# A filter block loaded and folded in two parts, nine small additions moved to GpSimd, eleven warm-up matmuls for fifteen, and a new order, in a gated long-convolution and token-mixing kernel

## The chip, the cores and the metric

One core of one Trainium2 chip runs the kernel. The metric is the device time of one execution in microseconds (us). The engines are TensorE (PE in the profile; its weight loads are listed apart as PEld), VectorE (DVE), ScalarE (ACT) and GpSimd (POOL). SyncE (SP) only issues DMAs here, and POOL issues a few of its own. All arrays are bfloat16; sums are made in float32.

## The reference, cut to what matters

S = 2048 positions, D = 640 channels, F = 1536 hidden units, a shift convolution of 4 taps.

```
x = A_q
g = sigmoid((x * gate_w).sum(-1))
# branch a: shift convolution, product, long causal convolution over S, product
k_shift = sum over t of k_pad[:, t:t+S, :] * shift_k[:, 3-t]
kv      = k_shift * v
y       = irfft(rfft(kv_pad) * rfft(ssm_k_pad)) + kv * ssm_D      # per channel, length 2S
a       = q * y
# branch b: layer norm over D, then an MLP over the positions
h = (x - mean) / sqrt(var + 1e-5)
u = gelu(einsum("bsd,sf->bdf", h, w1) + b1)
b = transpose(einsum("bdf,fs->bds", u, w2) + b2)
out = g * a + (1 - g) * b
```

## The kernel before, in words

**Long convolution.** The 2048 positions are cut into four blocks of n = 512, and so is the filter `ssm_k`. A block's transform is a product with cosine and sine tables on PE. The tables TFc, TFs, AFc and AFs are made in the kernel: GpSimd writes the rows of integers `frow` (iota), DVE multiplies them by a column and takes the result modulo the period (`idx`, L660, four operations for TFc/TFs and two for AFc/AFs), ACT takes sines. Two further small columns, `nyt`, come from DVE (L661).

For filter block i the steps are:

- `wnat_load` brings the block in, 128 channels x (5 columns of blocks x 512 values), 640 KB, into the buffer `wnat{i}`, which has 16 values more that a memset on POOL makes zero (they are read past the end by the reversed view).
- `w_turn(i)` folds it on DVE: `fw` is the block read forward and `bw` the block read backward; two wide operations (sum and difference, 128 x 1280 each) give the two parts e = 0 and e = 1 of `en`, and four operations of one value per row and block (`sam`) correct their first columns.
- For i = 0 and 1, PE turns `en` by products with the identity `idp`: four groups (e, k), each of five 128 x 128 products into one PSUM tile, which ACT or DVE copies to `eo` (`evict`, L1006 on DVE). For i = 0 the last group also adds `drow` (ssm_D). For i = 2 and 3 a DMA turns `en`.
- `w_freq(i)` multiplies `eo` by the tables (eight groups on PE), and ACT copies the results to `W{i}` (`Wo` for i = 1).

The product side is alike: `kv_block(i)` (shift convolution on PE with the small diagonal tables `dg`, evictions `ks`, a DMA that turns them to `kt`, products with v on DVE), `a_freq`, then `pair(j, m)` (products of A and W summed in Z, all DVE), `inverse(m)` (PE) and `epilogue(m)`.

**Token MLP.** The rows of x come in nine groups: tiles 0 and 1 alone, then pairs (2,3), (4,5), ... (14,15); a group is named by its first tile (ln0, ln1, ln2, ...). For each tile DVE takes the statistics of two halves (L919) and combines them (L921, buffer `mv`). For each group an addition of 1e-5 gives `vpe` (L923 through the helper at L660, DVE) and a power of -0.5 gives `rstd` (L924, POOL). Then DVE normalises (L661) or, for four of the tiles, ACT does, after a small DVE operation (`nmr`). `mlp1(s)` does two of the 12 tiles of F at a time (six sets), `mlp2(q)` two of the 16 tiles of S (eight sets, each with its own 768 KB block of w2, loaded through two buffers `w2_0` and `w2_1`).

**Ends.** The last scatter to the output (L728) takes tile 15, whose product (`mlp2(7)`, reversed weights `w2r1`) is made some groups before PE's end; the very last groups on PE are tile 14's, and DVE finishes that tile with two fused operations (L1327) from PSUM and two stores.

**Order.** Every operation is first recorded with a number in `_Plan`, and then issued in the hand-written list `ORDER` (L433 to L470). Each engine, SP's queue included, runs its own part of that list in the list's order; `_Tracker` puts in the semaphore waits for operands, and for buffers that are still in use. Each PE group takes one of four PSUM tiles (`pp0` to `pp3`) and holds it till its eviction. So what an engine waits for, it waits for in place: everything behind it in its own part of the list waits too. The numbers called cost and pr in the code (`cost=0.07`, `pr`) do not set the order here; the list does.

**Warm-up.** At the start PE multiplies a constant `wz` with itself, 15 matmuls of 128 x 512 (`NWARM`, L490 and L778), which nothing reads.

The part of the list that each engine sees at the start, by what it works on (wt1 = turning block 1, wf1 = its tables, and so on):

- PE: warm-up; the four turning groups of block 1; six table groups of block 1; the `drow` group of block 0; two more of block 1's; the other three of block 0; three shift convolution groups (cv0); block 0's table groups; then cv1 and the first set of the MLP.
- DVE: constants; four `idx`; statistics of ln1; an `idx` and two `nyt` and another `idx`; block 1's difference and sum; then statistics of ln14, ln12 and ln6 among block 1's corrections; block 0's folds as the 37th and 38th operation.
- POOL: three constants and `ncol_i` first, `frow` as the 9th and 10th operation.
- SP: x of ln1, block 1 of the filter (640 KB), `shd`, x of ln14, ln12 and ln6, `drow`, block 0 of the filter, x of ln8, and further x.

Of the kernel before, what the change touches and what calls it, by code (L numbers as in the profile page):

```python
# [8 lines left out]
BF16 = mybir.dt.bfloat16  # L9
# [3 lines left out]
ALU = mybir.AluOpType  # L13
# [409 lines left out]
def _checked(items, offs, base, top):  # L423
# [49 lines left out]
def _build(nc, A_q, A_k, A_v, A_shift_k, A_ssm_k, A_ssm_D, B_x, B_w1, B_b1, B_w2, B_b2, gate_w, out):  # L473
# [16 lines left out]
    NWARM = 15  # L490

    with ExitStack() as es:
# [14 lines left out]
        def buf(name, shape, dtype, t0, t1):  # L507
            spec.append((name, list(shape), dtype, t0, t1))
# [56 lines left out]
        for i in range(P):  # L565
            buf(f"wnat{i}", [128, DC * n + 16], BF16, (0, 0, 42, 52)[i], (26, 28, 52, 60)[i])
# [103 lines left out]
        def memset(ap, val, pr, eng="POOL"):  # L670
            return vop(eng, 0.03 + nel(ap) / 1200.0, lambda e: e.memset(ap, val), [], [ap], pr, kind="ms")  # L671
# [234 lines left out]
        for gi, (t0, cnt) in enumerate(groups):  # L906
# [16 lines left out]
            ts(b["vpe"][:, sl], b["mv"][:, sl, 1], 1e-5, None, ALU.add, None, pr, cost=0.07)  # L923
# [45 lines left out]
        def wnat_load(i, pr):  # L969
            dma(b[f"wnat{i}"][:, 0:DC * n].rearrange("p (c v) -> p c v", c=DC), dram(A_ssm_k, i * n, [[S, 128], [128 * S, DC], [1, n]]), f"wnat{i}", pr)  # L970

        brow = b["brow"]
# [35 lines left out]
        def w_turn(i):  # L1008
            plan.tag = f"wt{i}"
            wn = b[f"wnat{i}"]  # L1010
            en = b[f"en{1 if i == 1 else 0}"]
            eo = b[f"eo{i % 2}"]
            wnat_load(i, (-300.0, -280.0, -240.0, -180.0)[i])
            memset(wn[:, DC * n:DC * n + 16], 0.0, 0.3)

            def sam(v):
                return bass.AP(tensor=wn, offset=v, ap=[[DC * n + 16, 128], [n, DC], [1, 1]])

            fw = bass.AP(tensor=wn, offset=256, ap=[[DC * n + 16, 128], [-256, 2], [n, DC], [1, 128]])
            bw = bass.AP(tensor=wn, offset=256, ap=[[DC * n + 16, 128], [256, 2], [n, DC], [-1, 128]])  # L1020
            pr = 1.0 + 0.1 * i
            fo = i in FOLD
            tt(en[:, 0, :, :, :], fw, bw, ALU.add, pr)
            copy(en[:, 0, 0, :, 0:1], sam(256), pr, "DVE")
            tt(en[:, 1, :, :, :], fw, bw, ALU.subtract, pr)
            copy(en[:, 0 if fo else 1, 1, :, 0:1], sam(0), pr, "DVE")
            tt(en[:, 1 if fo else 0, 1, :, 0:1], sam(384), sam(128), ALU.add, pr)
            tt(en[:, 1, 0, :, 0:1], sam(384), sam(128), ALU.subtract, pr)
            if i in WDMA:
                dma(eo[:, :, :, :].rearrange("p e k (c d) -> p (e k c) d", c=DC),  # L1030
                    en[:, :, :, :, :].rearrange("p e k c u -> p (e k c u)"), f"wt{i % 2}", pr, turn=True)
            else:
                for e in range(2):
                    for k in range(2):
                        p_ = _PS()
                        xd = i == 0 and e == 1 and k == 1
                        mms = [(p_, c * 128, 128, en[:, e, k, c, :], ident, not xd or c in (0, 4), not xd) for c in range(DC)]
                        if xd:
                            mms += [(p_, c0, cn, ident[0:1, :], b["drow"][:, c0:c0 + cn], False, True)
                                    for c0, cn in ((0, 512), (512, 128))]  # L1040
                        pe([p_], mms, pr, cost=0.285 + (0.35 if xd else 0.0))
                        evict(WEV[i][2 * e + k], eo[:, e, k, :], p_)
# [395 lines left out]
```

## Time and profile before

| | |
|---|---|
| median of 3 runs | 190.6 us (190.5 to 192.65) |
| the profiled execution | 190.98 us |
| its span (first to last recorded instruction) | 189.2 us |
| PE busy | 178.8 us, 95% of the span, 1590 matmuls |
| DVE busy | 175.5 us, 93%, 246 instructions |
| ACT busy | 125.5 us, 66% |
| POOL busy | 35.2 us, 19% |
| DMA | 40.37 MB, mean 213 GB/s; HBM read 26.03 MB, written 7.54 MB |
| granted TensorE clock | 1.00 throughout |

How to read the profile's lines in the prediction: the rows of the stretches give for each stretch of the span its length, then for PE, PEld, DVE, ACT and POOL the busy time in it with the number of instructions in brackets, then the granted clock, the mean busy share of the DMA engines (a transfer counted where it ran can bring a stretch above 1), and GB/s. A row of the chain gives the time at which a step of the chain starts (us), how much of the chain it takes, the engine, what it writes and the line; "xN" are N instructions in a row. A row of the timeline gives start, busy time, engine, line, operation, out<-in, shapes, count, and in square brackets the idle time before it with what ended it. A row of the groups gives line, engine, operation, out<-in, shapes and count, then busy us and mean ns of one, then the idle time before them with what ended most of it.

### The profile page before, as it was taken

The page shows a single profiled execution, that of the slowest core. Times are in us where ns is not written, and L with a number is a line of the kernel's source. Part 1 is how long each engine was busy: PE and PEld are TensorE (multiplying, and loading weights), DVE is VectorE, ACT ScalarE, POOL GpSimd, SP SyncE. Part 2 cuts the span into 40 slices and gives each one's busy share as a digit, 9 for nine tenths or more (in the row PEclk, how much of TensorE's full clock was granted, in tenths as well). Part 3 has the DMA queues.
Part 4 walks back from the last instruction along what each step waited for, and adds up shares of the span by engine and source line. Part 5 has one row for each costly group of instructions (what it writes and reads, how often), then busy time and mean ns, then how long its engine had stood idle before and what let it go on. Part 6 is the DMA issues. An engine that isn't in the chain of part 4 may idle for free.

```text
span 189.2 us, 3940 instructions
## 1 busy us (share of the span) xinstructions
PE 178.8 (95%) x1590; PEld 123.0 (65%) x1590; DVE 175.5 (93%) x246; ACT 125.5 (66%) x202; POOL 35.2 (19%) x68
## 2 busy tenths in 40 slices
PE   7778899999999999999999999999999899999992
PEld 2345666566667757777767777777667577777771
DVE  7999999999999999999899999999999999997352
ACT  4978999787699489439823047706778482495930
POOL 8366076610000000101000000000005003110732
PEclk9999999999999999999999999999999999999999
DMA  5999999798996876787948998997988976979992
GB/s 155 315 325 272 130 152 282 221 222 190 236 326 129 196 202 181 151 248 164 232 67 221 231 243 197 219 242 205 309 280 224 225 226 221 232 215 240 175 166 69
DMA packets 81094, 40.37 MB, mean 213 GB/s; under 512 B 40051, under 2 KB 80884, under 8 KB 81076
## 3 DMA queue, kind: packets, MB, share of 16 engines
q1 hardware_dynamic: 78340, 37.18, 78.5%
q0 software_dynamic: 2736, 2.95, 9.3%
q8 instruction: 12, 0.20, 0.4%
q14 instruction: 6, 0.05, 0.1%
HBM read 26.03 MB, written 7.54 MB: 177 GB/s over the span
## 4 chain that ended last, share of the span: by engine, by line
PE 61%; DVE 22%; ACT 4%; issue 4%; DMA 4%; POOL 2%; POOLq 1%; DVEq 0%
PE pp L311 61%; DVE stats L919 6%; DMA w<-in_B_w_dram 4%; DVE v L653 3%; DVE en L653 3%; DVE es L653 2%; DVE idx L660 2%; DVE W L653 2%; ACT pq L691 1%; POOL rstd L924 1%; ACT xe L691 1%; DVE h L661 1%; DVE eo L1006 1%; DVE mv L921 1%; DVE A L653 1%
## 5 line engine op out<-in xcount | busy, mean ns | idle before, releaser
L311 PE MATMUL pp<-h,w 128*128 128x320 bf16 x384 | 57.1, 299 | 0.2
L311 PE MATMUL pp<-gT,w 128*128 128x320 bf16 x336 | 48.4, 299 | 0.9 <-DMA w<-in_B_w_dram 0.9
L311 PEld LDWEIGHTS pp<-h,w 128*128 128x128 bf16 x384 | 36.8, 98 | 15.9 <-issue 1.8
L311 PEld LDWEIGHTS pp<-gT,w 128*128 128x128 bf16 x336 | 32.6, 98 | 14.0 <-DMA w<-in_B_w_dram 1.4
L653 DVE TENSOR_TENSOR tt<-A,W 128x3840 bf16<-128x3840 bf16 (+2 forms) x16 | 27.8, 1738 | 0.3
L691 ACT ACTIVATE A<-pp 128x640 bf16<-128x640 f32 x32 | 21.3, 700 | 9.3 <-PE pp L311 9.3
L653 DVE TENSOR_TENSOR Z<-Z,tt 128x3840 bf16<-128x3840 bf16 (+1 forms) x14 | 26.2, 1868 | 0.2
L262 POOL DMA_DIRECT2D out_dram<-xe x3 | 3.8, 1252 | 73.0 <-DVE Z L653 68.4
L691 ACT ACTIVATE o<-pp,c,omg 128x640 bf16<-128x640 f32 x13 | 11.2, 881 | 6.8 <-PE pp L311 6.4
L691 ACT ACTIVATE ks<-pp 128x512 bf16<-128x512 f32 (+1 forms) x24 | 11.1, 518 | 6.1 <-PE pp L311 6.1
L691 ACT ACTIVATE gT<-pp,bf 128x640 bf16<-128x640 f32 x12 | 9.4, 792 | 8.2 <-PE pp L311 8.1
L691 ACT ACTIVATE xe<-xe,gg 128x640 bf16<-128x640 bf16 x16 | 12.7, 827 | 2.4 <-DMA xe<-rows_q 1.2
L919 DVE BATCH_NORM_STATS2 stats<-x 128x6 f32<-128x320 bf16 x32 | 13.7, 472 | 0.0
L653 DVE TENSOR_TENSOR Z<-A,W 128x3840 bf16<-128x3840 bf16 x6 | 12.8, 2154 | 0.9 <-PE pp L311 0.8
L691 ACT ACTIVATE pq<-pp 128x640 bf16<-128x640 f32 x16 | 10.3, 702 | 4.8 <-PE pp L311 4.8
L671 POOL MEMSET W<- 1x640 bf16 x4 | 2.7, 665 | 50.9 <-ACT nq L691 49.6
L691 ACT ACTIVATE W<-pp 128x640 bf16<-128x640 f32 x18 | 12.0, 722 | 0.1
L653 DVE TENSOR_TENSOR W<-W 128x2560 bf16<-128x2560 bf16 x8 | 11.9, 1486 | 0.0
L653 DVE TENSOR_TENSOR y<-pq 128x1280 bf16<-128x1280 bf16 (+1 forms) x10 | 6.6, 688 | 4.5 <-ACT pq L691 4.5
L311 PE MATMUL pp<-kT,dg 64*64 64x256 bf16 x320 | 10.5, 271 | 0.3 <-ACT Wo L691 0.3
L311 PE MATMUL pp<-eo,TFc 128*128 128x320 bf16 x48 | 8.9, 300 | 1.1 <-ACT TFc L691 1.1
L653 DVE TENSOR_TENSOR Z<-Z 128x1280 bf16<-128x1280 bf16 (+1 forms) x16 | 9.9, 653 | 0.1
(147 smaller groups left out, 303.6 us busy)
## 6 DMA issues: line engine op xcount, KB each, us to landing
w<-in_B_w_dram SPq DMA_DIRECT2D x24, 256.0 KB, 4.1
w<-in_B_w_dram SPq DMA_DIRECT2D x8, 768.0 KB, 5.1
wnat<-in_A_ssm_k_dram SPq DMA_DIRECT2D x4, 640.0 KB, 5.7
x<-in_A_q_dram SPq DMA_DIRECT2D x7, 320.0 KB, 6.3
out_dram<-o SPq DMA_DIRECT2D x6, 320.0 KB, 6.1
v<-in_A_v_dram SPq DMA_DIRECT2D x4, 320.0 KB, 4.5
rows_q<-in_A_q_dram SPq DMA_DIRECT2D x8, 160.0 KB, 3.2
xe<-in_A_q_dram SPq DMA_DIRECT2D x4, 320.0 KB, 5.8
```

What stands on the lines that cost most here:

```text
L262: ins = engobj.dma_start(out_ap, in_ap, accum_op=ALU.add)
L311: ins = self.nc.tensor.matmul(ps_ap, lhsT=lhsT, rhs=rhs, start=start, stop=stop)
L653: return vop(eng, c, lambda e: e.tensor_tensor(out_, in0, in1, op), [in0, in1], [out_], pr, kind="tt")
L660: return e.tensor_scalar(out_, in0, s1, None, op0=op0)
L661: return e.tensor_scalar(out_, in0, s1, s2, op0=op0, op1=op1)
L671: return vop(eng, 0.03 + nel(ap) / 1200.0, lambda e: e.memset(ap, val), [], [ap], pr, kind="ms")
L691: return e.activation(out_, src, func, **kw)
L919: vop("DVE", 0.393, (lambda o_, i_: lambda e: e.bn_stats(o_, i_))(o_, i_), [i_], [o_], pr, kind="bn")
L921: vop("DVE", 0.11, (lambda o_, i_: lambda e: e.bn_aggr(o_, i_))(o_, i_), [i_], [o_], pr, kind="ba")
L924: vop("POOL", 0.7, (lambda o_, i_, e_: lambda e: e.tensor_tensor(o_, i_, e_, ALU.pow))(b["rstd"][:, sl], b["vpe"][:, sl], bc(c_mh, [[8, 12 ...
L1006: vop("DVE", 0.74, lambda e: e.tensor_copy(dst, src()), [src], [dst], 0.3, ps=[p_], kind="ev")
```

## The change

- **Block 1 of the filter in two parts.** A new function `wnat_part` loads columns of blocks 0 to 2 (384 KB) and 3 to 4 (256 KB) with two DMAs. The buffer `wnat1` is 16 values longer: the second part begins 16 values later, and a second memset on POOL makes the gap zero. `w_turn(1)` does its six fold operations once for each part, twelve in all, on 3/5 and 2/5 of the values. The four turning groups on PE become eight (three products and two), two to one PSUM tile, which is copied out after the second. The memsets are recorded ahead of the loads.
- **vpe on POOL.** The nine additions of 1e-5 (L923) run on GpSimd, ahead of the powers that it runs already.
- **NWARM** is 11, not 15.
- **ORDER** is new from end to end: 865 operations, not 853. By engine, at the start:
  - PE: warm-up; the `drow` group of block 0 first, then its other three turning groups; then block 1's groups in halves (columns 0 to 2, then 3 to 4) mixed with table groups of both blocks and with cv0; cv1's first group stands right ahead of the MLP's first groups.
  - DVE: constants; four `idx`; two `nyt`; statistics of ln14 and ln0 among two `idx`; block 1's sum and difference of columns 0 to 2 as the 15th and 16th operation; block 0's folds as the 24th and 28th, with the corrections that its first PE group needs up to the 32nd; then block 1's columns 3 to 4 and the remaining corrections.
  - POOL: `frow`'s second half first, its first half fifth; the powers go in the order ln14, ln0, ln2, ln4, ln12, ln1, ln10, ln6, ln8 (before: ln1, ln14, ln2, ln10, ln12, ln0, ln4, ln6, ln8).
  - SP: x of ln14, `drow`, block 1 columns 0 to 2, x of ln0, block 0, `brow`, x of ln4, block 1 columns 3 to 4, `shd`, x of ln2, ln12, ln8, ln6, ln10, and x of ln1 after the first `kT`.
  - Later: on SP w2's block for q = 4 stands ahead of the two `rows_o0` stores (before: behind them), and w2's block for q = 2 stands, as before, right behind the turn of `kt1`, but ahead of that turn there is another of the three loads of v2 than before, and both wait for it. Behind tile 15's last PE group stand four PE groups of four weight tiles each (before: three).

The diff without the list:

```diff
-    NWARM = 15
+    NWARM = 11
...
-            buf(f"wnat{i}", [128, DC * n + 16], BF16, (0, 0, 42, 52)[i], (26, 28, 52, 60)[i])
+            buf(f"wnat{i}", [128, DC * n + (32 if i == 1 else 16)], BF16, (0, 0, 42, 52)[i], (26, 28, 52, 60)[i])
...
-            ts(b["vpe"][:, sl], b["mv"][:, sl, 1], 1e-5, None, ALU.add, None, pr, cost=0.07)
+            ts(b["vpe"][:, sl], b["mv"][:, sl, 1], 1e-5, None, ALU.add, None, pr, eng="POOL", cost=0.25)
...
+        def wnat_part(i, c0, c1, pr):
+            o0 = c0 * n + (16 if c0 else 0)
+            dma(b[f"wnat{i}"][:, o0:o0 + (c1 - c0) * n].rearrange("p (c v) -> p c v", c=c1 - c0),
+                dram(A_ssm_k, i * n + c0 * 128 * S, [[S, 128], [128 * S, c1 - c0], [1, n]]), f"wnat{i}_{c0}", pr)
...
-            wnat_load(i, (-300.0, -280.0, -240.0, -180.0)[i])
-            memset(wn[:, DC * n:DC * n + 16], 0.0, 0.3)
...
+            cuts = ((0, 3), (3, DC)) if i == 1 else ((0, DC),)
+            WR = DC * n + 16 * len(cuts)
+            if i == 1:
+                memset(wn[:, 3 * n:3 * n + 16], 0.0, 0.3)
+            memset(wn[:, WR - 16:WR], 0.0, 0.3)
+            for c0, c1 in cuts:
+                if i == 1:
+                    wnat_part(i, c0, c1, -290.0 + c0)
+                else:
+                    wnat_load(i, (-300.0, -280.0, -240.0, -180.0)[i])
+                cn = c1 - c0
+                o0 = c0 * n + (16 if c0 else 0)
...
+                fw = bass.AP(tensor=wn, offset=256 + o0, ap=[[WR, 128], [-256, 2], [n, cn], [1, 128]])
+                bw = bass.AP(tensor=wn, offset=256 + o0, ap=[[WR, 128], [256, 2], [n, cn], [-1, 128]])
+                tt(en[:, 0, :, c0:c1, :], fw, bw, ALU.add, pr)
...
+                tt(en[:, 1, :, c0:c1, :], fw, bw, ALU.subtract, pr)
...
+                ps = {}
+                for c0, c1 in cuts:
+                    for e in range(2):
+                        for k in range(2):
+                            if c0 == 0:
+                                ps[e, k] = _PS()
+                            p_ = ps[e, k]
...
+                            mms = [(p_, c * 128, 128, en[:, e, k, c, :], ident, not xd or c in (0, 4), not xd) for c in range(c0, c1)]
...
+                            pe([p_], mms, pr, cost=0.057 * (c1 - c0) + (0.35 if xd else 0.0))
+                            if c1 == DC:
+                                evict(WEV[i][2 * e + k], eo[:, e, k, :], p_)
```

More of the change, by code (lines that the diff above doesn't have):

```diff
@@ L970, in wnat_load @@
             dma(b[f"wnat{i}"][:, 0:DC * n].rearrange("p (c v) -> p c v", c=DC), dram(A_ssm_k, i * n, [[S, 128], [128 * S, DC], [1, n]]), f"wnat{i}", pr)
+        def wnat_part(i, c0, c1, pr):
+            o0 = c0 * n + (16 if c0 else 0)
+            dma(b[f"wnat{i}"][:, o0:o0 + (c1 - c0) * n].rearrange("p (c v) -> p c v", c=c1 - c0),
+                dram(A_ssm_k, i * n + c0 * 128 * S, [[S, 128], [128 * S, c1 - c0], [1, n]]), f"wnat{i}_{c0}", pr)
+        def wnat_load(i, pr):
+            dma(b[f"wnat{i}"][:, 0:DC * n].rearrange("p (c v) -> p c v", c=DC), dram(A_ssm_k, i * n, [[S, 128], [128 * S, DC], [1, n]]), f"wnat{i}", pr)
         brow = b["brow"]
@@ L1012, in w_turn, with sam @@
             eo = b[f"eo{i % 2}"]
-            wnat_load(i, (-300.0, -280.0, -240.0, -180.0)[i])
-            memset(wn[:, DC * n:DC * n + 16], 0.0, 0.3)
[L1016 to L1020, printed above, removed]
             pr = 1.0 + 0.1 * i
             fo = i in FOLD
[L1023 to L1028, printed above, removed]
+            cuts = ((0, 3), (3, DC)) if i == 1 else ((0, DC),)
[10 more added lines that the diff above has]
+                o0 = c0 * n + (16 if c0 else 0)
+                def sam(v):
+                    return bass.AP(tensor=wn, offset=v + o0, ap=[[WR, 128], [n, cn], [1, 1]])
+                fw = bass.AP(tensor=wn, offset=256 + o0, ap=[[WR, 128], [-256, 2], [n, cn], [1, 128]])
+                bw = bass.AP(tensor=wn, offset=256 + o0, ap=[[WR, 128], [256, 2], [n, cn], [-1, 128]])
+                tt(en[:, 0, :, c0:c1, :], fw, bw, ALU.add, pr)
+                copy(en[:, 0, 0, c0:c1, 0:1], sam(256), pr, "DVE")
+                tt(en[:, 1, :, c0:c1, :], fw, bw, ALU.subtract, pr)
+                copy(en[:, 0 if fo else 1, 1, c0:c1, 0:1], sam(0), pr, "DVE")
+                tt(en[:, 1 if fo else 0, 1, c0:c1, 0:1], sam(384), sam(128), ALU.add, pr)
+                tt(en[:, 1, 0, c0:c1, 0:1], sam(384), sam(128), ALU.subtract, pr)
             if i in WDMA:
@@ L1032, in w_turn @@
             else:
[L1033 to L1042, printed above, removed]
+                ps = {}
[5 more added lines that the diff above has]
+                            p_ = ps[e, k]
+                            xd = i == 0 and e == 1 and k == 1
+                            mms = [(p_, c * 128, 128, en[:, e, k, c, :], ident, not xd or c in (0, 4), not xd) for c in range(c0, c1)]
+                            if xd:
+                                mms += [(p_, d0, dn, ident[0:1, :], b["drow"][:, d0:d0 + dn], False, True)
+                                        for d0, dn in ((0, 512), (512, 128))]
+                            pe([p_], mms, pr, cost=0.057 * (c1 - c0) + (0.35 if xd else 0.0))
+                            if c1 == DC:
+                                evict(WEV[i][2 * e + k], eo[:, e, k, :], p_)
         ORD = (0, 1, 2, 3)
```

73 rows, old and new, of the table ORDER are left out of this document.

## The prediction

> **What bounds the kernel now.** I read the busy time by stretch first, then the chain of work that ended last in order of time, then the timeline of the first 36 us. The stretches (columns: length, then busy us and instructions of PE, weight loads, DVE, ACT, POOL; granted clock; DMA share; GB/s):
>
> ```profile
> 0.00:8.22 8.22, 5.84 (x15) 1.95 (x15) 6.50 (x20) 5.34 (x8) 5.63 (x34) 1.00 0.70 215
> 8.22:25.00 16.78, 13.95 (x179) 9.74 (x180) 16.78 (x55) 14.85 (x27) 6.74 (x9) 1.00 1.14 254
> 25.00:50.00 25.00, 24.32 (x231) 15.58 (x229) 24.86 (x53) 21.23 (x36) 10.09 (x13) 1.00 0.92 213
> 50.00:141.00 91.00, 91.00 (x852) 64.82 (x850) 89.61 (x72) 55.45 (x95) 1.24 (x2) 1.00 0.88 215
> 141.00:150.00 9.00, 8.11 (x61) 5.65 (x59) 9.00 (x8) 7.00 (x12) 2.38 (x2) 1.00 0.89 222
> 150.00:185.54 35.54, 35.54 (x262) 25.30 (x260) 27.97 (x42) 21.59 (x28) 8.12 (x8) 1.00 0.85 200
> 185.54:189.20 3.66, 0.00 (x1) 0.00 (x0) 0.74 (x2) 0.00 (x0) 1.01 (x1) 1.00 0.27 90
> ```
>
> PE's useful work starts at 8.22 and ends at 185.54. In those 177.32 us it idles 2.83 + 0.68 + 0.89 = 4.4 us, so its work is 172.9 us. The 5.84 us before are warm-up matmuls on a constant. DVE is full as well until about 170. The chain says the same by place:
>
> ```profile
> 6.48 1.69 DVE en L653 x3
> ...
> 49.74 92.22 PE pp L311 x858
> 141.96 6.96 DMA w<-in_B_w_dram
> 148.92 0.05 issue
> 148.96 23.55 PE pp L311 x172
> ```
>
> DVE sets the pace of the front (filter folds, layer norm statistics), PE that of everything from 49.7 on, with one DMA wait (the 0.89). The change removes no PE work but warm-up. So I do the sum on PE: when its useful work starts, how long it idles, at which rate it runs, and what follows its end.
>
> **Term 1: PE's first useful group.** Before, it transposes block 1 as soon as that is folded (8.22). In the new order PE begins with block 0's group (second part, second half, with drow), which needs block 0's two folds and two corrections, and DVE has more ahead of those. Path shares of such instructions, from the chain:
>
> ```profile
> 1.87 2.21 DVE idx L660 x4
> ...
> 5.54 0.49 DVE idx L660
> 6.02 0.07 DVE nyt L661
> 6.09 0.40 DVE idx L660
> ...
> 9.09 0.08 DVE en L653
> ...
> 9.22 1.19 DVE stats L919 x3
> 10.41 0.24 DVE mv L921 x2
> ...
> 12.65 1.48 DVE en L653 x2
> ...
> 17.66 0.72 DVE eo L1006
> ```
>
> The four index operations ended at 4.08; the two frow iotas now stand first and fifth on POOL instead of ninth and tenth, so I take 3.9. Then, on DVE: 2 nyt (0.14), 7 statistics at 0.40 (2.8), 2 index operations (0.89), the two folds of block 1's first three columns of blocks (0.74 each for five; 3/5 with the fixed part kept, 0.47: 0.94), 3 aggregates (0.36), block 0's two folds (1.48), four small ones (id2, the AFs column, two corrections at 0.08: 0.3). Together 6.9, so 10.8 against 8.22: **+2.6 us**. Do the loads carry it?
>
> ```profile
> 0.00:5.00 5.00, 3.93 (x10) 1.42 (x11) 3.60 (x11) 2.19 (x3) 3.98 (x26) 1.00 0.53 156
> 5.00:10.00 5.00, 3.55 (x27) 1.65 (x25) 4.68 (x18) 4.93 (x8) 1.66 (x8) 1.00 1.00 326
> ```
>
> Up to block 0's last byte SP now issues x 320, part one 384, x 160, block 0 640 KB: 1.5 MB. At these rates 0.78 MB are there by 5 us, the rest 2.3 us later, at 7.3; DVE asks for block 0 at 8.6. Part one (0.7 MB) is there by 4.7, asked for at 5.8. I cost the loads at nothing; the cover is about one us each.
>
> **Term 2: the idle after that.** Before, 2.83 us between 8.22 and 25, because block 1's groups run dry. Now both blocks' groups are mixed from the start. After the first four groups (1.9 us, to 12.7) PE needs block 1's last-corrected half: 5 small operations, two folds of the two remaining columns (0.35 each), one eviction (0.72), two more corrections, 2.05 us of DVE after 10.8, so 12.85: a gap of 0.2. From there DVE is ahead of PE for every group that I followed. The evictions on ACT remain a limit with four PSUM buffers; for those I leave 0.5, a choice. 2.83 becomes 0.7: **-2.1**.
>
> **Term 3: the rate.** The weight loads show when each warm-up matmul starts:
>
> ```profile
> 1.07 5.84 PE L311 MATMUL pp<-wz 128*128 128x512 bf16 x15 [1.07 <-DVE wz L671]
> ...
> 5.32 0.15 PEld L311 LDWEIGHTS pp<-wz 128*128 128x128 bf16 x1 [0.28 <-issue]
> ...
> 5.74 0.15 PEld L311 LDWEIGHTS pp<-wz 128*128 128x128 bf16 x1 [0.28 <-issue]
> ...
> 6.10 0.32 PEld L311 LDWEIGHTS pp<-wz 128*128 128x128 bf16 x2 [0.21 <-issue]
> ...
> 8.22 0.28 PEld L311 LDWEIGHTS pp<-idp,en 128*128 128x128 bf16 x5 [1.81 <-DVE en L653]
> ```
>
> One matmul in 0.42 us until about 6.0, then one in 0.2, though the clock column says 1.00 throughout: PE runs its first 4.9 us at half rate. Then comes a pause of 1.3 us, and the transposes after it run at full rate (five loads in 0.28). Eleven warm-ups end at 5.74, before the doubling, and then PE pauses for 5.1 us until 10.8. The trace has no such pause. Bounds: nothing lost (as after the pause of 1.3), or another 4.9 us at half rate, 2.45 us of work. The new state (never at full rate, pause four times as long) is nearer the start than the short pause, so I take the half rate. PE is busy 83% there (13.95 of 16.78), so 2.0, less the 0.7 of idle that a slower PE fills: **+1.3**.
>
> The Trainium skill (TensorE: Matmul & The Clock Gate, Part 1: The HAM clock gate) says that about 3.4 us of sustained activity open the full clock and an idle window of about 3.4 us closes it. The two spacings and the 1.3 us pause agree with it; a pause over 3.4 is not in this trace. By that rule the start at 10.8 is cold for 3.4 to 6.8 us, an estimated loss of 1.7 to 3.4 us before slack, and the sum would be about half a us higher.
>
> **Term 4: GpSimd's additions.** Nine additions leave DVE (0.03 to 0.13 us of path each, about 0.7) and the split adds six DVE instructions (four at 0.08, two fixed parts at 0.07, 0.46). DVE nets -0.3, which moves only PE idle that I have counted. On POOL the trace has no such addition; its neighbours:
>
> ```profile
> L924 POOL TENSOR_TENSOR rstd<-vpe,cst 128x2 f32<-128x2 f32 x7 | 5.3, 809 | 7.0 <-DVE vpe L660 6.9
> L924 POOL TENSOR_TENSOR rstd<-vpe,cst 128x1 f32<-128x1 f32 x2 | 1.1, 568 | 0.1
> L668 POOL CAST gwc<-bf 128x5 bf16<-128x5 f32 x1 | 2.4, 2395 | 0.0
> ...
> L668 POOL CAST hcol<-hcol_i 128x2 f32<-128x2 int32 x1 | 0.4, 357 | 0.0
> ```
>
> Between ln4's last aggregate and ln8's first normalisation DVE has 8 statistics, 6 aggregates, 9 normalisations and 2 nmr, 7.2 us; POOL has five powers at 0.81, one at 0.57 and six additions in it, 4.6 + 6v. It is late when v is over 0.43. Bounds of v: 0.1 (a memset's duration, a gain of nothing) and 2.4 (the 128x5 cast, 12 us late). The nearest in shape and type is the 128x2 cast, 0.36: 6.8 of 7.2, **0**. The extra memset of the gap waits for nothing on POOL.
>
> The Trainium skill (GPSIMD Engine Reference, 1. Specifications) says GpSimd shares SBUF interfaces with VectorE. The powers at 0.57 and 0.81 may show that; the sum stays as it is.
>
> **Term 5: the middle.** 0.68 + 0.89. The 0.89 was w2's block for q = 4, queued on SP behind two rows_o0 stores that waited for DVE; now it stands ahead of them, and the wait goes. Late next is the block for q = 2: it stands behind the kt transpose, which now stands behind a v load that waits for a later group of PE; about 0.7. I take 1.57 to 1.4: **-0.2**.
>
> **Term 6: the end.**
>
> ```profile
> 183.75 1.79 PE L311 MATMUL pp<-gT,w 128*128 128x320 bf16 x12
> 183.95 0.88 ACT L691 ACTIVATE o<-pp,c2x,omx 128x640 bf16<-128x640 f32 x1 [2.92 <-PE pp L311]
> ...
> 185.27 1.01 DVE L1327 SCALAR_TENSOR_TENSOR xe<-pp,omg,xe 128x320 bf16<-128x320 f32 x2
> 185.64 1.01 POOL L728 DMA_INDIRECT out_dram<-xe,rev  x1 [3.53 <-DVE xe L653]
> ```
>
> The last scatter hangs on PE's group that ends three groups of four before PE's end; in the new order four groups stand behind it, 0.54 us more. The other end (last fused operation, store) follows PE's end and limits the gain: **-0.5**.
>
> **Sum.** +2.6 - 2.1 + 1.3 + 0 - 0.2 - 0.5 = +1.1 us. It is made against the profiled execution (span 189.2, 190.98 us with what lies around it, 0.4 above the median of 190.6). On the median: **191.7 us**.
>
> **Rivals.** (B) The rate is full from 10.8 on: term 3 is 0, 190.4 us. For it: a shorter pause did no harm. Against: the doubling is not reached by 5.74. (C) The order leaves PE no idle time and the rate is full: 10.8 + 172.9 + 0.2, then 3.1, is 187.0 of span, -2.2: 188.4. Against: the old order, made in the same way, left 4.4. (D) GpSimd becomes the bound of the layer norm: an addition takes about 1.2 us beside DVE's two-input work, POOL is 4.6 us late with rstd, of which 1.5 hide behind PE's own lag: 194.8. It decides from v = 1.1 on. For it: the 2.4 us cast; against: every other small POOL row. (E) The change does not do what it says: the split gives no earlier fold that PE uses, since PE starts with block 0. That is in my sum already; if the fold of part one also waited for its load, PE would start another 1 us later: 192.7.
>
> **Chances.** Forecast 0.45, B 0.22, C 0.10, D 0.10, E 0.08; 0.05 for a wait that I have not seen. The measurement of this kernel can tell about 2% from no change, 3.8 us: faster means below 186.8, slower above 194.4. B, C, E and the forecast lie within; D and half of the unseen lie above. Faster 0.04, within 0.82, slower 0.14. The range goes from near C (188.4) to the line at 194.4, short of D: 188.6 to 194.4; the forecast's own is 190.4 to 193.
>
> **What would show it.** PE's first matmul on en at about 10.8 (term 1 wrong if at 8). The starts of its matmuls over 320 columns just after: 0.27 us apart is the half rate, 0.135 the full. Idle PE between 11 and 25 under 1 us (term 2). On POOL, additions near 0.36 and no DVE wait for rstd (term 4). PE waits for w2 at q = 2, not q = 4 (term 5). PE's end to the span's end 3.1 (term 6). Wrong altogether if PE idles several us after 50, where I followed only the main producers.

## The result and the profile after

The changed kernel takes 191.78 us (median of 22 runs, 190.83 to 193.43), the kernel before 190.41 us (22 runs). The ratio is 1.0062 with a 95% interval of 1.0044 to 1.0081: slower by 0.6%, some 1.2 us. The profiled execution of the changed kernel took 191.72 us with a span of 189.9 us, against 190.98 and 189.2. The two profiled executions thus lie 0.7 us apart, the medians 1.4: the account from the profile below covers the 0.7.

The stretches of the changed kernel, cut at PE's first and last useful group as in the prediction (columns as there):

```profile
0.00:12.07 12.07, 4.71 (x11) 1.49 (x12) 9.64 (x33) 9.03 (x13) 9.68 (x41) 0.87 0.82 249
12.07:25.00 12.93, 11.96 (x150) 9.15 (x154) 11.80 (x41) 10.53 (x18) 3.31 (x8) 0.86 1.07 242
25.00:50.00 25.00, 24.76 (x255) 16.72 (x248) 24.66 (x51) 20.99 (x37) 10.88 (x18) 1.00 0.81 189
50.00:141.00 91.00, 90.97 (x850) 64.67 (x848) 89.43 (x72) 55.47 (x95) 1.24 (x2) 1.00 0.92 215
141.00:150.00 9.00, 8.60 (x64) 5.99 (x63) 8.97 (x10) 4.74 (x7) 2.36 (x2) 1.00 0.94 226
150.00:186.62 36.62, 36.62 (x270) 26.11 (x268) 31.02 (x43) 25.71 (x35) 8.60 (x9) 1.00 0.91 207
186.62:189.90 3.28, 0.00 (x1) 0.00 (x0) 0.69 (x2) 0.00 (x0) 0.57 (x1) 0.98 0.32 108
```

PE's useful work starts at 12.07 instead of 8.22 and ends at 186.62 instead of 185.54. Between them PE idles 0.97 + 0.24 + 0.03 + 0.40 = 1.64 us (before 4.4), and is busy 172.9 us, as before. But the clock column is no longer 1.00. Cut at the places where it changes:

```profile
5.48:8.90 3.42, 0.30 (x2) 0.00 (x0) 3.42 (x11) 3.28 (x6) 2.74 (x8) 1.00 1.00 327
8.90:12.07 3.17, 0.00 (x0) 0.01 (x1) 2.65 (x12) 2.78 (x5) 3.08 (x10) 0.50 1.10 328
12.07:15.72 3.65, 3.65 (x28) 2.83 (x29) 2.55 (x11) 2.22 (x3) 1.84 (x4) 0.50 1.27 288
```

The warm-up opens the full clock at 5.48 and ends at 5.78; after 3.4 us with 0.30 us of work in them the grant falls to 0.50 at 8.90, and PE does its first 3.65 us of useful work at half rate.

Busy time alone doesn't tell where the time went, because at half rate PE is busy as well. So I compare when each kernel starts its n-th useful matmul; both have 1575. From the traces' starts, us:

| kernel | 1st | 101st | 401st | last | span |
|---|---|---|---|---|---|
| before | 8.23 | 20.94 | 48.61 | 185.24 | 189.2 |
| changed | 12.07 | 23.58 | 50.43 | 186.32 | 189.9 |
| changed, 36 warm-up matmuls (e1) | 11.68 | 21.94 | 48.42 | 184.14 | 187.7 |
| the same again (e10) | 11.94 | 22.17 | 49.23 | 185.37 | 188.9 |
| new front, old rest (e3) | 11.52 | 23.22 | 51.17 | 188.34 | 192.3 |
| old front, new rest (e4) | 8.23 | 20.93 | 48.60 | 184.55 | 188.1 |
| e1 without the split (e6) | 12.32 | 23.07 | 49.96 | 185.51 | 189.0 |
| before, 11 warm-up matmuls (e7) | 8.23 | 20.94 | 48.61 | 184.44 | 188.4 |

The changed kernel is 3.84 us late at its first matmul, 1.8 at the 401st and 1.1 at the last; 0.4 more comes back in the tail. Each row is one execution. Two executions of one kernel (e1 and e10) differ by 0.8 us at the 401st and by 1.2 at the last, so a difference of that size between two rows needs the runs beside it.

### The profile page after: what moved, and what is told of

Same layout as the page of the kernel before. It is cut to its first block, busy times and chain, and to the rows that moved or that the text cites. A ratio compares the mean times of both kernels' runs of the same rounds, so it can differ in the third digit from the quotient of the medians.

```text
span 189.9 us, 3933 instructions
## 1 busy us (share of the span) xinstructions
PE 177.6 (94%) x1586; PEld 124.1 (65%) x1586; DVE 176.2 (93%) x243; ACT 126.5 (67%) x202; POOL 36.6 (19%) x78
## 4 chain that ended last, share of the span: by engine, by line
PE 82%; DVE 6%; DMA 4%; POOL 3%; ACT 2%; issue 1%; DVEq 0%; POOLq 0%
PE pp L311 82%; DMA w<-in_B_w_dram 4%; DVE stats L920 3%; DVE idx L661 1%; POOL v L723 1%; DVE dg L1004 1%; POOL rstd L925 1%; ACT TFs L692 1%; ACT ks L692 1%; ACT o L692 0%; DVE eo L1015 0%; ACT adx L692 0%; DVE xe L1351 0%; POOL vpe L661 0%; POOL flp L661 0%
## 5 line engine op out<-in xcount | busy, mean ns | idle before, releaser
L311 PE MATMUL pp<-h,w 128*128 128x320 bf16 x384 | 57.8, 299 | 0.0
L311 PE MATMUL pp<-idp,en 128*128 128x128 bf16 x40 | 4.3, 277 | 6.3 <-DVE en L654 6.3
L311 PEld LDWEIGHTS pp<-kT,dg 64*64 64x64 bf16 x320 | 8.2, 105 | 3.0 <-issue 1.6
```

The costliest lines, as they stand in the source:

```text
L311: ins = self.nc.tensor.matmul(ps_ap, lhsT=lhsT, rhs=rhs, start=start, stop=stop)
```

## The experiments

The experiments ran on two chips. The kernel before took 191.13 us on the first (e1 to e4), 190.54 on the second (e5 to e8) and 190.53 there again (e9 to e11). The ratios are to the kernel before on the same chip; I hold these against each other, not the microseconds.

**e1: warm-up up to the first group.**

```diff
-    NWARM = 11
+    NWARM = 36
```

> The changed kernel with 36 warm-up matmuls instead of 11, so that PE is busy until about its first useful group at 12.07 us; nothing else differs. Theory A (the clock falls back in the pause, and PE's work behind it is paid for at half rate): the granted clock is 1.00 from about 6 us on, the transposes' matmuls start 0.053 us apart instead of 0.107, and the 1.8 us that the half rate cost (3.65 us of it, half lost) come back: 190.0 us against 191.8 for the changed kernel. Rival B (VectorE sets the pace of the front, so a faster PE only waits longer): the clock is full as well, but PE then waits for the fold dg, which ends at 23.07 whatever PE does; only the 1.1 us come back that VectorE waited for PE's groups: 190.7 to 191.8 us.

Measured: 189.7 us, 0.9947 of the kernel before (0.9914 to 0.9979). A second measurement beside another experiment (e10) follows below. Its stretches, then a row of its weight loads, then the same row of the changed kernel:

```profile
0.00:11.68 11.68, 9.95 (x36) 3.96 (x37) 9.64 (x33) 8.72 (x12) 9.29 (x37) 1.00 0.81 242
11.68:25.00 13.32, 12.26 (x171) 9.08 (x172) 13.29 (x47) 12.37 (x24) 5.61 (x14) 1.00 1.06 255
...
sum 187.70, PE 181.38 PEld 125.55 DVE 175.86 ACT 126.08 POOL 36.85; mean PE 25.91 PEld 17.94 DVE 25.12 ACT 18.01 POOL 5.26
```

```profile
11.68 0.28 PEld L311 LDWEIGHTS pp<-idp,en 128*128 128x128 bf16 x5 [1.15 <-DVE en L669]
```

```profile
12.06 0.45 PEld L311 LDWEIGHTS pp<-idp,en 128*128 128x128 bf16 x5 [7.03 <-DVE en L669]
```

Five loads take 0.28 us in e1 and 0.45 in the changed kernel, full and half rate. In e1 PE is busy 181.38 - 9.95 = 171.4 us behind its first group, 1.5 less than the 172.9 of the changed kernel (171.4 to 171.6 in all five executions of the new order at full clock: e1, e5, e6, e10, e11): that is the half rate. Theory A is shown. Rival B falls: at the 401st matmul e1 is 2.0 us ahead of the changed kernel, 0.4 of it from an earlier first group, and PE's wait for dg did not grow (0.8 us for 1.0). In e10's execution the lead is 1.2 us, which alone would not exclude rival B; but by the ratios its range is 1.0005 to 1.0062, and both measurements lie below it. VectorE did not hold PE back by as much as that, since it evicts two of block 0's groups itself and had waited for them; that wait (1.1 us in the changed kernel's list of waits) is gone in e1's.

**e2: fifteen warm-up matmuls, as before.**

```diff
-    NWARM = 11
+    NWARM = 15
```

> The changed kernel with 15 warm-up matmuls, as many as before; nothing else differs. Theory A (it is the pause before the first useful group that costs the clock, not the number of warm-up matmuls): the warm-up ends near 7 us, 5 us of pause are left, the granted clock still falls to 0.5 and lasts into 15 us: 191.4 to 191.8 us, no different from the changed kernel. Rival C (eleven warm-up matmuls are too few to open the clock, fifteen keep it open): the clock stays at 1.0 as in the kernel before, and the time is 190.0 to 190.7 us.

Measured: 191.54 us, 1.0024 (1.0001 to 1.0046), on the same chip as e1. Its clock falls in the same way:

```profile
5.00:10.00 5.00, 1.37 (x7) 0.40 (x5) 3.94 (x11) 3.81 (x7) 3.29 (x12) 1.00 1.01 319
10.00:15.00 5.00, 2.50 (x19) 1.80 (x20) 4.50 (x19) 4.11 (x7) 4.25 (x10) 0.68 1.32 332
15.00:20.00 5.00, 5.00 (x34) 3.50 (x32) 4.39 (x15) 3.09 (x6) 0.00 (x0) 0.64 0.95 235
```

So the four warm-up matmuls that the change took away are not what costs; the pause behind them is. Theory A holds and rival C falls: e2 is 0.8% behind e1. It stands 0.4% better than the changed kernel's 1.0062, which is from another measurement, with intervals that just meet; whether the four matmuls give that much stays open.

**e3 and e4: the two lists crossed at about 46 us.** Numbers of operations are translated between the two kernels.

```diff
-ORDER = new list
+ORDER = new list[:341] + [the other operations, in the old list's order]     # e3, code of the changed kernel
...
-ORDER = old list
+ORDER = old list[:329] + [the other operations, in the new list's order]     # e4, code of the kernel before
```

> The changed kernel (split, GpSimd's additions, 11 warm-up matmuls) with the new order for its first 341 operations, to about 46 us, and the old order for the rest. Theory A (the new front loses 1.8 us by 48 us of PE's work, the new rest gives 1.1 of it back: 0.7 in waits, 0.4 at the end): the old rest keeps the loss, less what its own wait of 0.9 us for w2 takes up: 191.6 to 192.5 us, not under the changed kernel's 191.8. Rival D (the old rest takes up the lag of the front just as well, its waits for VectorE and loads being set by other engines): 190.4 to 191.3 us.

> The kernel before (no split, additions on VectorE, 15 warm-up matmuls) with the old order for its first 329 operations, to about 46 us, and the new order for the rest. Theory A (the new rest is worth 0.7 us in waits and 0.4 us at the end by itself): 190.4 - 1.1 = 189.3 us. Rival D (the new rest gives nothing by itself; it only ran in the shadow of a front that was late): 190.2 to 190.6 us, no different from the kernel before.

Measured: e3 193.27 us, 1.0114 (1.0078 to 1.015); e4 190.15 us, 0.9961 (0.9928 to 0.9994). Two of e4's stretches:

```profile
141.00:150.00 9.00, 9.00 (x68) 6.49 (x67) 9.00 (x9) 6.50 (x9) 2.34 (x2) 1.00 0.93 185
...
184.85:188.10 3.25, 0.00 (x1) 0.00 (x0) 0.69 (x2) 0.00 (x0) 0.57 (x1) 1.00 0.32 107
```

The 0.89 us of idle between 141 and 150 is gone and the tail is 3.25 for 3.66. The runs give 0.4%, 0.75 us, with an interval that ends just short of no change. The tail's 0.4 us is shown: it is 3.2 to 3.3 us in every execution with the new rest and 3.6 to 3.7 in every one with the old. The 0.7 us on PE (184.55 for 185.24, last column but one of the table) is not: e7 has the old rest, and its last matmul starts at 184.44. The same stretch in e7:

```profile
141.00:150.00 9.00, 9.00 (x67) 6.28 (x66) 9.00 (x8) 7.13 (x12) 2.38 (x2) 1.00 0.91 229
```

The idle 0.89 us is gone there too, without the new list. Of five profiled executions with the old rest (before, e3, e7, e8, e9) only one has it. So theory A is shown for the tail and open for the rest.

e3 is slower than the changed kernel by 0.5%, with intervals that just meet. By its ratio it stands at the top of theory A's range (1.0114 of 190.41 is 192.6 us); the 193.27 is above it because that chip is slower. In its profiled execution the clock is at 0.50 from 10.03 to 16.86, so that 5.3 us of PE's work run at half rate and not 3.65; that is 0.85 us more lost, of the 2.0 us by which its last matmul is behind the changed kernel's. Part of the rest is waiting. Two of its waits (us in all, times, longest):

```profile
PE pp L311 <- DVE es L654: 1.3, 1, 1.3
...
PE pp L311 <- DVE v L654: 0.8, 2, 0.5
```

The same two lines of the kernel before:

```profile
PE pp L311 <- DVE v L653: 0.3, 1, 0.3
PE pp L311 <- DVE es L653: 0.2, 1, 0.2
```

Behind the new front the old rest waits 2.1 us for VectorE's products where it waited 0.5. Rival D falls in e3, and in e4 by a narrow margin.

**e5, e10 and e11: the additions back on VectorE, at full clock.**

```diff
-            ts(b["vpe"][:, sl], b["mv"][:, sl, 1], 1e-5, None, ALU.add, None, pr, eng="POOL", cost=0.25)
+            ts(b["vpe"][:, sl], b["mv"][:, sl, 1], 1e-5, None, ALU.add, None, pr, cost=0.07)
```

> The changed kernel with 36 warm-up matmuls, and the nine additions of 1e-5 back on VectorE at the same places of the list. To be compared with the changed kernel with 36 warm-up matmuls (189.7 us, ratio 0.9947 to the kernel before). Theory A (the additions take 0.24 us on GpSimd, under the 0.43 from which it would be late, and 0.1 us each on VectorE; neither is waited for): the same within 0.3 us, 189.4 to 190.0. Rival E (GpSimd's powers, 0.89 us each now for 0.81, are late with rstd): taking the additions off it gains 0.5 to 1 us, 188.7 to 189.2. Rival F (VectorE paces the front, so its nine additions, 0.7 us, cost in full): 190.2 to 190.5.

> The changed kernel with 36 warm-up matmuls a second time, beside the next kernel on the same chip, to hold the two against each other: 189.4 to 190.2 us, ratio 0.993 to 0.998 to the kernel before.

> The same with the nine additions back on VectorE, a second time. In its first profiled execution 1.0 of the 1.6 us by which its PE was late at 48 us came from a load of the filter that landed 0.9 us later than in the other kernel's, which the additions can't have caused. Theory A (the additions cost nothing on either engine, and the first difference of 0.9 us was the landing): the two kernels agree within 0.3 us when beside each other. Rival F (VectorE paces the front and the additions cost there what they take): 0.5 to 1.0 us slower than the kernel beside it again, also where the loads land at the same time.

Measured: e5 190.61 us, 1.0002 (0.9979 to 1.0025); then side by side e10 (additions on GpSimd) 190.32 us, 0.998 (0.9956 to 1.0004), and e11 (on VectorE) 190.5 us, 1.0004 (0.9977 to 1.0031). Both pairs (e1 and e5, which ran on different chips, and e10 and e11) lean to GpSimd, by 0.55% and 0.24%, with intervals that meet or overlap. In the profiled executions of the second pair the one with the additions on VectorE was ahead at the 401st matmul (48.81 against 49.23). What the move of the additions is worth in the new order stays open, between nothing and 1 us. e10 also says that e1 beats the kernel before by something between 0.2% and 0.5%, and only the first measurement of it beyond its interval.

**e6: without the split, at full clock.**

```diff
# the code of the kernel before, with the additions on GpSimd, 36 warm-up matmuls and the new list;
# block 1's load at the first part's place in ORDER, its folds and turning groups at the second part's
```

> The changed kernel with 36 warm-up matmuls and without the split: block 1 loaded by one DMA of 640 KB at the place of the first part, folded by six operations and turned by four groups at the places of the second part. To be compared with 189.7 us (ratio 0.9947). Theory A (PE begins with block 0, so the early fold of block 1's first three columns gives PE nothing; without it VectorE reaches block 0's folds 0.9 us earlier, but waits for block 0's load, which lands near 9.7): PE's first group stays at 11.5 to 12.3 us and the time at 189.3 to 190.0 us. Rival G (the split feeds PE with block 1's groups between block 0's and spares it a stretch of idle time): 190.3 to 191.2 us.

Measured: 191.35 us, 1.0039 (1.0015 to 1.0064). The same kernel with the split has 0.9947 (e1) and, on this chip, 0.998 (e10). Theory A falls, and rival G holds for the time: the split in this list is worth 0.6 to 0.9%, 1.1 to 1.8 us. Folding the whole block at the first part's place wasn't run. Whom PE waits for in e6 behind its first group, the longest:

```profile
PE pp L311 <- DVE dg L995: 0.9, 1, 0.9
PE pp L311 <- DVE eo L1006: 0.8, 1, 0.8
```

and whom VectorE waits for there:

```profile
DVE stats L919 <- DMA x<-in_A_q_dram: 0.9, 1, 0.9
DVE en L653 <- DMA wnat<-in_A_ssm_k_dram: 0.8, 1, 0.8
```

Without the early fold VectorE has less to do while the loads come (it waits 0.9 and 0.8 us for them, in the stretch where it sets the pace). The loads also come later: the x and block 0 for which it waits now stand behind 640 KB of block 1 on the queue and not behind 384 KB (issued at 2.12 in both, that x landed at 7.25 in the changed kernel and at 8.1 in e6). And VectorE does the whole fold of block 1 (two operations of 0.8 us, from 12.31 on) when PE has already begun, so that the evictions behind it come late and PE waits 0.8 us for them. The wait for dg is there in the changed kernel too. How the price divides between the later loads and the later fold is not shown.

**e7 and e8: the warm-up of the kernel before.**

```diff
-    NWARM = 15
+    NWARM = 11     # e7
+    NWARM = 22     # e8
```

> The kernel before with 11 warm-up matmuls instead of 15; nothing else differs. Theory A (the clock is judged over stretches of 3.4 us; with 11 the warm-up ends at 5.8 and a stretch with a pause of 2.4 us follows): the granted clock falls to 0.5 for 3.4 us or more after the first transposes at 8.22, PE, which idles 2.8 us there anyway, loses 0.3 to 1 us of it: 190.7 to 191.6 us. Rival H (a pause of 2.4 us is too short to lose the clock): 190.2 to 190.6 us and a clock of 1.00.

> The kernel before with 22 warm-up matmuls instead of 15, so that PE is busy until about its first useful group at 8.22 us. Theory A (its clock is full from 6 us on already): no change, 190.2 to 190.6 us. Rival I (in other executions than the one profiled the old kernel's pause of 1 to 2 us loses the clock too, which is where its runs of 191 to 193 us come from): the median falls by 0.3 to 0.8 us, and fewer runs lie above 191.

Measured: e7 190.83 us, 1.0031 (0.9997 to 1.0065); e8 190.97 us, 1.0 (0.9964 to 1.0035). e7's clock:

```profile
4.40:7.80 3.40, 0.84 (x4) 0.20 (x2) 3.04 (x10) 3.33 (x6) 1.64 (x9) 1.00 0.97 291
7.80:11.22 3.42, 2.99 (x24) 2.45 (x24) 3.42 (x16) 2.91 (x6) 0.67 (x4) 0.50 1.09 362
```

Here too the clock falls after a stretch of 3.4 us with little work (0.84), for one such stretch. But the 101st and the 401st matmul start at 20.94 and 48.61 as before: the old front idles enough behind its first groups to hide it. So theory A was right on the clock; its price stays open. The median of 0.3% lies in its range, with an interval from nothing to 0.65%, and the profiled execution shows no loss. e8 shows no change, as theory A says, and six of its twelve runs lie above 191 us, so rival I falls.

**e9: the additions alone, in the old order.**

```diff
-            ts(b["vpe"][:, sl], b["mv"][:, sl, 1], 1e-5, None, ALU.add, None, pr, cost=0.07)
+            ts(b["vpe"][:, sl], b["mv"][:, sl, 1], 1e-5, None, ALU.add, None, pr, eng="POOL", cost=0.25)
```

> The kernel before with the nine additions of 1e-5 on GpSimd at the same places of the old list; nothing else differs. Theory A (0.24 us on GpSimd and 0.1 us on VectorE, neither waited for): the same within 0.3 us, 190.2 to 190.7. Rival E (in the old order seven powers stand back to back on GpSimd from 24.84 to 30.17; seven additions of 0.24 make that 1.7 us longer, and the normalisations wait): 191.0 to 191.8 us and a wait of VectorE for rstd. Rival F (VectorE paces the front, so 0.7 us less on it is 0.7 us gained): 189.6 to 190.0.

Measured: 192.47 us, 1.01 (1.0061 to 1.014). VectorE's waits:

```profile
DVE nmr L661 <- POOL rstd L924: 0.9, 1, 0.9
...
DVE h L661 <- POOL TS L671: 0.7, 1, 0.7
DVE h L661 <- POOL rstd L924: 0.6, 1, 0.6
```

and one of PE's, with the stretches around it:

```profile
PE pp L311 <- DMA kT<-in_A_k_dram: 2.3, 1, 2.3
```

```profile
25.00:28.50 3.50, 3.50 (x25) 1.82 (x22) 2.90 (x13) 3.50 (x7) 3.33 (x8) 1.00 1.45 90
28.50:31.05 2.55, 0.29 (x8) 0.18 (x11) 1.60 (x6) 2.55 (x5) 2.38 (x5) 1.00 0.85 103
31.05:34.46 3.41, 3.41 (x65) 2.71 (x61) 2.80 (x5) 1.83 (x4) 1.65 (x3) 0.50 0.93 251
```

VectorE waits 2.2 us for GpSimd in the layer norm (the middle row's memset stands right behind the last power), where it waited for none before: rival E holds, above its range, and the move for which the new order shows no loss costs 1% in the old. In the profiled execution a wait of PE for the turned load of k (2.3 us, and a stretch at half rate behind it) comes on top; why that load lands later is not settled, since the additions only touch GpSimd and VectorE. The half rate isn't the main cause of the loss: three of the six runs have a mean clock of 0.997 to 1.000, and they took 192.1 us.

## Why the prediction was right, point by point

The time (191.7 against 191.78) and the direction were right, and the clock was the right reason for the loss. The sum is right partly because errors in other steps cancel.

- **Term 1, PE's first group** (+2.6 predicted, +3.85 measured): two steps failed, VectorE's own path to block 0's fold, and "I cost the loads at nothing; the cover is about one us each". Three rows of VectorE:

```profile
3.26 0.92 DVE L661 TENSOR_SCALAR idx<-idx 128x512 int32<-128x512 int32 x2
...
5.23 0.49 DVE L661 TENSOR_SCALAR idx<-frow,hcol 128x512 int32<-128x512 int32 x1 [0.53 <-ACT adx L692]
...
9.74 0.84 DVE L654 TENSOR_TENSOR en<-wnat 128x1280 bf16<-128x1280 bf16 x1 [0.52 <-DMA wnat<-in_A_ssm_k_dram]
```

and of the DMA issues (KB, median us from issue to landing):

```profile
wnat<-in_A_ssm_k_dram SPq DMA_DIRECT2D x3, 640.0 KB, 6.6
...
wnat<-in_A_ssm_k_dram SPq DMA_DIRECT2D x1, 384.0 KB, 4.6
```

Part one, issued at 1.67, landed at 6.2 and not at 4.7; block 0 at 9.7 and not at 7.3, where VectorE waited 0.52 for it. I had taken the moment when the rows' GB/s add up to the bytes; the engine was let go 1.5 to 2.4 us after that. The Trainium skill (DMA: Bandwidth & Descriptors, Anatomy of one DMA) gives about 2 us of fixed cost for a DMA that GpSimd issues, most of it the confirmation that the last byte has landed. These loads are issued by SP, for which that section gives no figure, and their delay isn't fixed here: in e3, with the same front, VectorE found block 0 landed at 9.20.

```profile
9.20 0.83 DVE L654 TENSOR_TENSOR en<-wnat 128x1280 bf16<-128x1280 bf16 x1
```

  VectorE's own path was short by 0.8: the four index operations ended at 4.18 and not at 3.9, and a later one waits 0.53 until ACT has read the buffer that it writes; I had counted VectorE's own work only. The two causes overlap, since VectorE would have waited longer for block 0 had it come there sooner. In e1 and e3, where the load was there in time, PE began at 11.68 and 11.52. So of the 1.25 us that term 1 lacked, 0.7 to 0.9 are VectorE's path and 0.4 to 0.55 the load of this execution.

- **Term 2, idle behind it** (-2.1 predicted): the idle that the rows show went from 2.83 to 0.97, -1.9. But at full clock (e1) PE's useful work is busy 171.4 us where the kernel before is busy 172.9, for the same matmuls. The difference lies in the first 401 of them. One of the groups, before and in e1:

```profile
L311 PE MATMUL pp<-eo,TFc 128*128 128x320 bf16 x48 | 8.9, 300 | 1.1 <-ACT TFc L691 1.1
...
L311 PE MATMUL pp<-eo,TFc 128*128 128x320 bf16 x48 | 8.5, 299 | 0.0
```

  The profile gives each the same 0.30 us in both kernels; what differs is how closely they follow each other. I conclude that the old front held 1.5 us of short waits which its busy share of 13.95 in 16.78 didn't show as idle, and that the new order took these as well. Terms 1 and 2 together were +0.5; at full clock they are -0.2 (48.42 against 48.61 at the 401st matmul), in e10's execution +0.6.
- **Term 3, the clock** (+1.3 predicted): right in kind and nearly in size. The half rate lasted 3.65 us and cost 1.5 us of busy time; e1 takes back 0.8 to 1.15% in the ratios. The 3.65, like the 6.1 in e2's execution and the 5.3 in e3's, agrees with the 3.4 to 6.8 us that the prediction worked out from the Trainium skill (TensorE: Matmul & The Clock Gate, Part 1: The HAM clock gate). Part of the spread of the changed kernel's runs goes with the clock: eight of the 22 have a mean clock of 0.982 and a median of 191.3 us, seven have 0.973 and 192.7 us, and 0.009 of some 190 us is 3.4 us at half rate more. Not all of it does: two runs with a mean clock of 1.000 took 191.72 and 192.15 us, and what they lost is not on record.
- **Term 4, GpSimd's additions** (0 predicted): right in the new order. The additions took 0.24 and 0.29 us, under the bound of 0.43, and nobody waited for rstd:

```profile
L925 POOL TENSOR_TENSOR rstd<-vpe,cst 128x2 f32<-128x2 f32 x7 | 6.2, 894 | 0.4
L661 POOL TENSOR_SCALAR vpe<-mv 128x2 f32<-128x2 f32 x7 | 1.7, 244 | 9.7 <-DVE mv L922 9.6
...
L661 POOL TENSOR_SCALAR vpe<-mv 128x1 f32<-128x1 f32 x2 | 0.6, 286 | 0.0
```

  The powers grew from 0.81 to 0.89. The bound on v was an argument about one order only; e9 shows the same additions late in another.
- **Term 5, the middle** (-0.2 predicted): 1.57 became 0.24 + 0.03 + 0.40 = 0.67, -0.9. The wait for q = 4 isn't there, as said, but the runs don't show that the move took it away: with the old rest it came in one execution of five (e4 above). The one forecast for q = 2 did not come. The 0.40 is the wait for q = 3's block, issued at 135.01; a wait of 0.4 to 0.8 us at this place stands in six of the eight executions with the new rest, and the prediction has none there.
- **Term 6, the end** (3.1 predicted): 3.28, -0.4.
- **Rivals B, C and D.** B and C need the full rate behind the pause, D an addition of 1.2 us; the half rate and the 0.24 to 0.29 us rule them out.
- **Rival E**, whose first half stood in my sum ("the split gives no earlier fold that PE uses"), is wrong: e6. PE's first group doesn't use the fold, but without the split the kernel is 0.6 to 0.9% slower: VectorE, which sets the pace, then waits for loads and folds later.

By PE's account the measured terms are +3.85, idle -2.76 in all, tail -0.38, busy 0.0: +0.7 in the span. The 0.0 hides two that cancel: +1.5 for the half rate and -1.5 for hidden waiting. That the forecast of 191.7 fell within 0.1 us of the median is luck: term 1 was 1.25 short, and term 5 and the hidden waiting gave that back and more.

## What to carry to other kernels

When a change makes PE's first useful group later, look at what PE does until then: warm-up that stops several us early is lost, and the work behind the pause is paid for at half rate, which a busy share can't show; compare when the n-th matmul starts instead. Reckon a load as there only when its issue-to-landing time is over, not when the bandwidth has moved its bytes. Before a wait in one profile is put into a sum, see whether a second execution of the same list has it. Moving small operations to an idle engine is free or not by the order alone: look for instructions that stand back to back on the receiving engine.

## What the runs showed of the hardware that was not expected

- The granted clock changes 3.4 us or a multiple of that apart (5.48, 8.90 and 15.72 in the changed kernel, 7.80 and 11.22 in e7, 31.05 and 34.46 in e9), at times that shift from one execution to the next. A stretch of that length with 0.30 us (changed kernel) or 0.84 us (e7) of PE work in it was followed by half rate, and so was one with a single pause of 2.3 us and 1.15 us of work in e9. In e2 a stretch with 1.45 us of work (4.92 to 8.33) was not; there the clock fell only after the next, empty one. The stretches of e9 and e2:

```profile
27.64:31.05 3.41, 1.15 (x14) 0.49 (x15) 2.46 (x9) 3.41 (x7) 3.17 (x6) 1.00 1.14 94
...
4.92:8.33 3.41, 1.45 (x7) 0.48 (x5) 2.27 (x5) 2.76 (x5) 2.18 (x8) 1.00 0.96 328
8.33:11.75 3.42, 0.00 (x0) 0.00 (x0) 3.42 (x12) 2.79 (x5) 2.78 (x8) 1.00 1.09 323
11.75:15.16 3.41, 2.67 (x21) 1.96 (x22) 2.75 (x14) 2.60 (x5) 2.58 (x7) 0.50 1.39 313
```

  A stretch with 2.99 us of work in 3.42, 20 small products with the identity and four with the tables (e7), opened the clock again.
- A filter block's landing moves by more than a us between executions in which SP issues it at the same time (1.67). Part one is asked for at about 6.4 us: it was there at 6.2 in the changed kernel, while in e5 VectorE waited 1.0 us for it and PE's first group came at 12.71 instead of e1's 11.68:

```profile
DVE en L654 <- DMA wnat<-in_A_ssm_k_dram: 1.0, 1, 1.0
```
